# Delta-rule attention and a GELU layer on one core: both tiles turned in one run, the last product in a bank of its own, and VectorE's order laid out anew

## The chip, the core and the metric

The kernel runs on one core of a Trainium2 chip. The core's engines work side by side, each on a queue of its own: TensorE (PE; PEld is its loading of weights) multiplies, VectorE (DVE), ScalarE (ACT) and GpSimd (POOL) work element by element, and SyncE (SP) issues the loads and stores. The metric is the device time of one execution in microseconds (us). Before the change it is 666.46 us, the median of three runs (665.81 to 667.63).

## The reference

`q`, `k`, `v` are (4, 8, 768, 48) and `beta` is (4, 8, 768), all float32. The output of the first part is the input of the second.

```python
k_n = k / (np.linalg.norm(k, axis=-1, keepdims=True) + 1e-06)
for t in range(S):                      # 768 tokens, in order
    y[:, :, t] = einsum('bhd,bhde->bhe', q[:, :, t], state)
    v_old = einsum('bhde,bhd->bhe', state, k_n[:, :, t])
    state = state + beta_t * einsum('bhd,bhe->bhde', k_n[:, :, t], v[:, :, t] - v_old)
x = y.transpose(0, 2, 1, 3).reshape(3072, 384)
h = x @ w_in                            # 384 x 2048
out = (0.5 * h * (1 + erf(h / sqrt(2)))) @ w_out        # 2048 x 384
```

## The kernel before

**Tiling.** The 768 tokens are cut into NC = 12 chunks `c` of 64. A tile, in the code a unit `u` = (c, a) with a = 0 or 1, holds the 64 tokens of a chunk for two of the four batches: 128 partitions. Inside a chunk the recurrence is solved by a triangular inverse, between chunks a state `St` is carried. Two chunks make a group `g`.

**What a chunk needs.** Its keys and queries are transposed (`Kt`, `Qt`: L348/L349 by TensorE and ScalarE, L354/L359 by VectorE). `grams` (psG, L369) multiplies keys with keys, `queries` (L405, P) keys with queries. The norms of the keys: `prep` calls `squares` (ScalarE squares into `ksq`, L277; VectorE adds up into `n`, L280) and takes a root on GpSimd; `finish` calls `factors` (four operations of VectorE, L264 to L268), which make beta over the squared norm, `gm`. `scale_v` (L331, GpSimd) scales v. The inverse of a group is made on VectorE: L437 and L442 lay out the blocks, then 30 pairs of L449 (`tmp`) and L451 (`Nu`) eliminate row by row, L460 (`XM`) and L464 (`Zf`) transpose back. Three "joins" (`join_run`, psJ, L541, with L553 on VectorE and the copies L520 on ScalarE) put the blocks together.

**State steps of a chunk.** `against_state` (psK, L615), `subtract` (L627 on ScalarE, `W` by L628 and L629 on VectorE), `solve` (psU, L645; ScalarE copies `U`), `outputs`: `use` (psY, L664 and L673), `next_state` (St, L678) and `read` (x, L688). Then `turn`, once a tile: TensorE transposes x by three matmuls (psX, L709), ScalarE copies them to `xT` (L710).

**The MLP of a chunk** works on `xT` with 256 tokens. From c = 2 on both layers are cut into blocks and multiplied by a scheme with fewer products, in which VectorE adds and subtracts blocks. First layer: per half b of the columns 11 products of about 0.9 us in the order P1, P5, P6, P2, R22, R11, P7, P3, R12, P4, R21 (L829, in `part_of_layer`). Between them are `mix_x` (L799: TX, needed by P5), the sums L852 and L853 after P6, L861 after P7, L872 after P4, and ScalarE's copies of partial sums into `pu` and its GELUs (L817). Second layer: seven products of 2.6 us in the order 1, 5, 2, 6, 4, 7, 3 (L774, in `two`; 3 is called V here). `mix` prepares operands: n = 1 is L888 (`S`, needed by product 5) and L889, n = 2 is L891, n = 3 is L893. `read2` adds up the results: L922 after 6; L925 (`p`), L926, L927, L931 and ScalarE's L930 after 7; L936 after 3. The weights' sums that this needs are made once, in `sum_of_w_in` (`Sw`), `sums_of_w` (`T`, L757) and `last_sum_of_w` (L761).

**Buffers.** PSUM is handed out by tags. "dn" has two buffers of two banks, used by the state steps, joins and grams; "mlp" has two of one bank, used by X and Y of the products; "sq" and "z" have one bank each after the start, used by V1, Z and the turns. In SBUF the tag "x" (tile x of `read`) has two buffers, "ksq" one.

**Order.** Each step has a due time in units of a stage, written by hand into `plan` by `at(first, last, steps)`, which spreads steps over a stretch in proportion to their weights. `emit` sorts all steps by due time and traces them. In the main part VectorE runs exactly in that order. The order on the other engines is set by a scheduler, except where `together` keeps matmuls in one run, `behind` chains the products of the MLP, and `keep` or `keep_in_program_order` holds instructions of ScalarE in the order they are traced.

**Stages.** Stage w runs the state steps of chunk w beside the MLP of chunk w−1; its start is here the first matmul of P1 of the MLP. Even stages have the three joins of a group and the grams of chunks w+2 and w+3, odd stages the most of an elimination. Chunks 0 to 2 form the start, in which weights are also decoded; after w = 11 only the MLP of c = 11 is left.

Of the kernel before, what the change touches and what calls it, by code (L numbers as in the profile page):

```python
# [16 lines left out]
def kernel(  # L17
# [28 lines left out]
    nc = tc.nc  # L46
# [223 lines left out]
    def squares(u, n, engine=None):  # L270
        kd = u.Kn[:, :, 0:D]
        if engine is nc.gpsimd:
            ksq = su.tile([128, H, D], F32, tag="w_e", name="ksq")
        else:
            ksq = wk.tile([128, H, D], F32, tag="ksq", name="ksq", bufs=1)
        if engine is None:
            nc.scalar.activation(ksq, kd, ACT.Square)  # L277
        else:
            engine.tensor_tensor(ksq, kd, kd, op=ALU.mult)
        nc.vector.tensor_reduce(n, ksq, axis=AX.X, op=ALU.add)  # L280
# [12 lines left out]
    def prep(c):  # L293
# [4 lines left out]
        if c > 3:  # L298
            ns[c] = wk.tile([128, NA, H], F32, tag="n", name="n", bufs=4)
# [10 lines left out]
    def finish(c):  # L310
        t = (c % 2) * NA
        factors(gms[c // 2][:, t:t + NA], beta_m[:, c], ns[c])
# [398 lines left out]

    def state_steps(c, first=(), second=()):
        us = [tiles[c, a] for a in range(NA)]
        steps = [(3.0, together, (against_state, us), *first),
                 (2.0, together, (solve, us), *second), (3.0, outputs, us)]
        return steps + [(0.5, turn, u) for u in us]
# [36 lines left out]
    def sums_of_w():  # L753

        for n, a, b in ((1, B12, B11), (2, B22, 1), (4, B21, 2)):
            T[n] = more[0].tile([128, FH, DH], F32, name=f"T{n}")
# [62 lines left out]
    def part_of_layer(c, b, n):  # L819
# [30 lines left out]
        elif n == "P6":  # L850
            product(fresh("Y1", "mlp", ps), S1[2], L1["T"][2], True)
            nc.vector.tensor_tensor(L1["Y1"], L1["Y1"], L1["pu"][:, 0], op=ALU.add)  # L852
            nc.vector.tensor_tensor(L1["pu"][:, 1], L1["Y1"], L1["pu"][:, 1], op=ALU.add)  # L853
# [19 lines left out]
        else:  # L873
# [3 lines left out]
            if b == NB - 1:  # L877
                keep(nc.scalar.activation, L1["last"], L1["last"], ACT.Gelu)
                for h in range(2):
                    mix(c, 1, h)  # L880

    def mix(c, n, h):
        fs = slice(h * FH // 2, (h + 1) * FH // 2)
        a11, a12, a21, a22 = (A[a][k][:, fs] for a in range(2) for k in range(2))
        if n == 1:
            if h == 0:
                W2["S"] = more[0].tile([128, FH, 128], F32, tag="S1", name="S1")
# [7 lines left out]
    def two(c, n):  # L895
# [9 lines left out]
        elif n == 6:  # L905
            W2["Y"] = ps.tile([128, 2, DH], F32, tag="mlp", name="psY2")
# [7 lines left out]
        else:  # L914
            W2["V"] = W2["Y"][:, 1] if c < NC - 1 else dn("psV2")[:, 0, 0:DH]
# [26 lines left out]
    def second_layer(c, n):  # L942

        two(c, n)
        if n in (1, 2):
            for h in range(2):
                mix(c, n + 1, h)
# [132 lines left out]
    def late():  # L1080
# [3 lines left out]
        for a in range(NA):  # L1084
# [3 lines left out]
            for c in range(5, NC, 2):  # L1088
                tiles[c, a].Kb = Kb

    plan = [at(c + 1 + 0.25 * (c == 1), c + 2 + 0.25 * (c == 0), ffn_steps(c)) for c in range(NC)]
# [6 lines left out]
    plan += [at(1.08, 1.5, sums), at(1.51, 1.511, [(1.0, prep, c) for c in (2, 3)]), at(1.65, 1.655, [(1.0, finish_both)]), at(3.072, 3.073, [(1.0, finish, 4)]), at(2.725, 2.726, [(1.0, queries, third)]),  # L1098
             at(1.12, 1.6, state_steps(1)),
# [9 lines left out]
             at(2.8, 2.985, state_steps(2)[1:]),  # L1109
             at(2.73, 2.731, [(1.0, prep, 4)]), at(2.8, 2.9, [(1.0, grams, [tiles[4, a] for a in range(NA)])])]  # L1110
    plan += [at(0.995, 1.0, [(1.0, load_v, 2)]), at(2.727, 2.728, [(1.0, sums_of_w)]), at(3.2, 3.21, [(1.0, last_sum_of_w)])]
    plan += [at(c + (0.99 if c == 2 else 0.958), c + (0.991 if c == 2 else 0.959), [(1.0, mix_x, c)]) for c in range(2, NC)]
# [4 lines left out]
    for c in range(4, NC):  # L1117
# [10 lines left out]
        t = c - (0.06 if c % 2 == 0 else 0.15)  # L1128
# [83 lines left out]
```

## Time and profile before

| | before |
|---|---|
| median of three runs | 666.46 us |
| the profiled execution | 667.54 us |
| its span | 665.5 us |
| clock granted to TensorE | 0.985 |
| start of P1 in stages 4, 5, 6, 7 | 226.96, 282.68, 328.22, 382.66 us |
| start of P1 in stages 8, 9, 10, 11, and of the last MLP | 428.20, 483.49, 529.02, 579.49, 624.09 us |

The profile is one execution. A group's line gives its line of code, engine, operation, result and operands, count, busy time, mean time of one in ns and how long its engine was idle just before, with what ended that. A line of the timeline gives start, duration, engine, line, operation and count; in brackets the idle time before it and the instruction that ended it. The waits list sums such idle times by the line that waited and the one that released it.

### The profile page before, as it was taken

What the parts mean: (1) busy time and instruction counts of PE and PEld (TensorE: products, weight loads), DVE (VectorE), ACT (ScalarE), POOL (GpSimd) and SP (SyncE); (2) the same over time, 40 slices, a digit from 0 to 9 for tenths busy, and PEclk for the clock granted to TensorE, in tenths of its full rate; (3) what the DMA queues carried; (4) which work ended last, traced back from release to release, by engine and by line L of the source; (5) the groups of instructions that cost most, each with busy time, mean ns of one, the idle gap of its engine ahead of it and who ended that gap; (6) DMA issues with size and microseconds to landing.
All of it is one profiled execution on the core that took longest, in us unless ns stands there. A gap on an engine that the chain in (4) does not pass through costs nothing.

```text
span 665.5 us, 22152 instructions
## 1 busy us (share of the span) xinstructions
PE 628.6 (94%) x9702; PEld 576.0 (87%) x9702; DVE 503.6 (76%) x1040; ACT 254.1 (38%) x587; POOL 72.5 (11%) x62
## 2 busy tenths in 40 slices
PE   6877999999799899999999999999999999999997
PEld 5666877766699899999999999998899999999997
DVE  7999999999599986769886769886778875445242
ACT  3367744623442146232146232145233144132230
POOL 4051400100411012101012101012101000000000
PEclk9977999999899999999999999999999999999999
DMA  8886654302433234421234321221221210100101
GB/s 126 184 253 176 124 168 119 48 1 52 70 54 56 47 42 76 58 40 26 54 46 76 55 40 27 54 33 26 34 41 27 46 29 2 25 3 2 25 1 25
DMA packets 158433, 39.79 MB, mean 60 GB/s; under 512 B 150016, under 2 KB 153216, under 8 KB 158336
## 3 DMA queue, kind: packets, MB, share of 16 engines
q1 hardware_dynamic: 155344, 36.94, 28.5%
q10 hardware_dynamic: 2992, 1.43, 1.0%
q8 instruction: 76, 1.25, 0.8%
q14 instruction: 21, 0.17, 0.1%
HBM read 33.62 MB, written 4.72 MB: 58 GB/s over the span
## 4 chain that ended last, share of the span: by engine, by line
PE 58%; DVE 29%; issue 4%; ACT 4%; DMA 3%; SPq 1%; POOL 0%; DVEq 0%; ACTq 0%; POOLq 0%
PE psX L774 8%; PE psY L774 8%; PE psY L829 8%; PE psX L829 6%; PE psH L732 4%; PE psZ L774 4%; PE psZ L829 4%; PE psV L829 3%; PE psO L746 3%; DVE tmp L449 3%; DVE Nu L451 3%; PE psK L615 3%; DMA Kp<-in_k_dram 2%; PE psG L369 2%; PE psJ L541 2%
## 5 line engine op out<-in xcount | busy, mean ns | idle before, releaser
L829 PE MATMUL psX<-xT,w_in_sb 128*128 128x128 f32 x480 | 65.6, 280 | 0.5 <-ACT pu L817 0.2
L451 DVE TENSOR_TENSOR Nu<-Nu,tmp 128x30 f32<-128x30 f32 (+9 forms) x180 | 59.8, 332 | 6.2
L449 DVE TENSOR_TENSOR tmp<-Nu 128x30 f32<-128x30 f32 (+9 forms) x180 | 60.3, 335 | 4.2
L829 PEld LDWEIGHTS psX<-xT,w_in_sb 128*128 128x128 f32 x480 | 59.5, 193 | 1.9 <-ACT pu L817 1.0
L774 PE MATMUL psY<-w_out_sb,G 128*128 128x192 f32 x304 | 54.1, 329 | 4.4 <-DVE p L925 3.8
L710 ACT COPY xT<-psX 128x384 f32<-128x384 f32 x24 | 11.4, 477 | 118.6 <-PE psX L709 118.5
L774 PE MATMUL psX<-w_out_sb,G 128*128 128x192 f32 x320 | 55.7, 327 | 0.0
L774 PEld LDWEIGHTS psY<-w_out_sb,G 128*128 128x128 f32 x304 | 49.1, 190 | 6.5 <-DVE p L925 6.5
L305 POOL TENSOR_TENSOR n<-n,half 128x16 f32<-128x16 f32 x10 | 30.0, 3001 | 220.7 <-DVE n L280 200.5
L774 PEld LDWEIGHTS psX<-w_out_sb,G 128*128 128x128 f32 x320 | 51.8, 190 | 0.3
L732 PE MATMUL psH<-xT,w_in_sb 128*128 128x256 f32 x192 | 45.1, 388 | 2.0 <-ACT G L734 1.9
L746 PE MATMUL psO<-w_out_sb,G 128*128 128x384 f32 x128 | 44.7, 493 | 0.4 <-DVE w_out_sb L235 0.4
L732 PEld LDWEIGHTS psH<-xT,w_in_sb 128*128 128x128 f32 x192 | 36.0, 192 | 9.1 <-ACT G L734 3.3
L829 PE MATMUL psY<-xT,w_in_sb 128*128 128x128 f32 x320 | 42.4, 275 | 0.0
L817 ACT COPY pu<-psZ 128x512 f32<-128x512 f32 x40 | 23.4, 584 | 41.2 <-PE psZ L829 31.1
L829 PEld LDWEIGHTS psY<-xT,w_in_sb 128*128 128x128 f32 x320 | 38.9, 192 | 0.1
L746 PEld LDWEIGHTS psO<-w_out_sb,G 128*128 128x128 f32 x128 | 23.4, 190 | 14.8 <-DVE w_out_sb L235 1.3
L852 DVE TENSOR_TENSOR psY<-psY,pu 128x512 f32<-128x512 f32 x20 | 14.0, 699 | 28.1 <-PE psY L829 28.1
L817 ACT ACTIVATE G<-G 128x512 f32<-128x512 f32 x40 | 25.2, 629 | 22.0 <-DVE G L861 21.1
L331 POOL TENSOR_TENSOR V<-V,n 128x384 f32<-128x384 f32 x18 | 17.3, 973 | 122.0 <-DMA V<-in_v_dram 98.6
L774 PE MATMUL psZ<-T,S 128*128 128x192 f32 x160 | 28.6, 332 | 1.6 <-DVE S L888 1.6
L893 DVE TENSOR_TENSOR G<-G 128x512 f32<-128x512 f32 x20 | 13.8, 692 | 20.5 <-PE psX L774 20.4
(171 smaller groups left out, 1325.4 us busy)
## 6 DMA issues: line engine op xcount, KB each, us to landing
Kp<-in_k_dram SPq DMA_DIRECT2D x76, 96.0 KB, 3.2
w_out_sb<-in_moe_w_in_dram SPq DMA_DIRECT2D x24, 256.0 KB, 4.5
w_raw<-in_moe_w_out_dram SPq DMA_DIRECT2D x16, 384.0 KB, 4.5
V<-in_v_dram SPq DMA_DIRECT2D x48, 96.0 KB, 3.2
out_dram<-o_sb SPq DMA_DIRECT2D x36, 96.0 KB, 2.2
Qp<-in_q_dram SPq DMA_DIRECT2D x64, 32.0 KB, 2.1
Qp<-in_q_dram SPq DMA_DIRECT2D x16, 96.0 KB, 4.2
Qp<-in_k_dram SPq DMA_DIRECT2D x32, 32.0 KB, 2.4
```

The costliest lines, as they stand in the source:

```text
L305: nc.gpsimd.tensor_tensor(flat, flat, half, op=ALU.pow)
L331: engine.tensor_tensor(u.V, u.V, ns[u.c][:, u.a].unsqueeze(2).to_broadcast([128, H, D]), op=ALU.mult)
L449: nc.vector.tensor_tensor(tmp, nu[:, j + 1:, j:j + 1].to_broadcast([128, n, j]), nu[:, j:j + 1, 0:j].to_broadcast([128, n, j]), op=ALU.mult)
L451: nc.vector.tensor_tensor(nu[:, j + 1:, 0:j], nu[:, j + 1:, 0:j], tmp, op=ALU.add)
L615: nc.tensor.matmul(u.psK[to, x, r, j, :], lhsT=(u.Qt if x else u.Kt)[rows, p, j, :], rhs=St[rows, u.a, p ^ r, j, :], start=True, stop=True)
L732: nc.tensor.matmul(psH, lhsT=w_in_sb[:, f // 2, m, f % 2 * 128:(f % 2 + 1) * 128], rhs=xTs[c][:, m, :], start=(m == 0), stop=(m == NM - 1))
L746: nc.tensor.matmul(u.psO, lhsT=G[:, f, u.a * 128:(u.a + 1) * 128], rhs=w_out_sb[:, f, :], start=(f == 0), stop=(f == NF - 1))
L774: nc.tensor.matmul(ps_, lhsT=lhs[:, f, :], rhs=rhs[:, f, :], start=first and f == 0, stop=f == FH - 1, skip_group_check=not first)
L817: tc.keep_in_program_order(fn(*args))
L829: nc.tensor.matmul(ps_[:, i], lhsT=lhs[:, f // 2, f % 2 * 128:(f % 2 + 1) * 128], rhs=rhs, start=first and i == 0, stop=True, skip_group_c ...
L852: nc.vector.tensor_tensor(L1["Y1"], L1["Y1"], L1["pu"][:, 0], op=ALU.add)
L893: nc.vector.tensor_tensor(a12, a12, a11, op=ALU.subtract)
```

## The change

1. **Norms.** `ksq` takes a buffer of the tag "x" in place of its own, and its ScalarE instruction is held in program order. The sums `n` of two chunks share one tile, and `finish` runs once a group on 128x32 elements, not once a chunk on 128x16.
2. **Turns.** The new `turns` transposes both tiles into one "dn" buffer by six matmuls in one run, followed by one copy of 128x768 on ScalarE, held in order. Chunks 1 and 2 keep a `turn` for each tile. `state_at` gives each state step a due time of its own; weights go.
3. **Sums of the second layer's weights.** `sum_of_w` makes T1 and T2 at 2.727; T4 and the last sum move to 3.595 (from 2.727 and 3.2).
4. **Steps cut out of the MLP.** L853 becomes `add_p5`; `mix(c, 1, 0)` and `mix(c, 3, ·)` get due times of their own. They had followed P6, R21 and product 2.
5. **Buffers.** `S` is written into the tile `pu`, no longer into a tile of its own under the same tag. The result of product 3 is in a "dn" buffer for every chunk, and no longer beside that of product 7.
6. **Due times.** Most steps on VectorE, ScalarE's copies of joins and grams (now in blocks of four or two), some loads and the norms are moved.

The scheduler's order on TensorE changes with it: product 5 of even stages comes after psU, psJ and psG; the six transposes of the turns stand between product 7 and product 3, which isn't interrupted any more; psK of even stages no longer breaks product P4. In the start, `use` of chunk 2 goes ahead of the last matmuls of the MLP of chunk 1 (psO, L746), the transposes L348 of chunk 3 behind P6, and P1 isn't interrupted.

```diff
         else:
-            ksq = wk.tile([128, H, D], F32, tag="ksq", name="ksq", bufs=1)
+            ksq = wk.tile([128, H, D], F32, tag="x", name="ksq")
         if engine is None:
-            nc.scalar.activation(ksq, kd, ACT.Square)
+            keep(nc.scalar.activation, ksq, kd, ACT.Square)
         else:
...
-        if c > 3:
-            ns[c] = wk.tile([128, NA, H], F32, tag="n", name="n", bufs=4)
+        if c > 3 and c % 2 == 0:
+            n = ns["pair"] = wk.tile([128, 2 * NA, H], F32, tag="n", name="n")
+            ns[c], ns[c + 1] = n[:, 0:NA], n[:, NA:]
...
     def finish(c):
-        t = (c % 2) * NA
-        factors(gms[c // 2][:, t:t + NA], beta_m[:, c], ns[c])
+        factors(gms[c // 2], beta_m[:, c:c + 2].rearrange("q c a h -> q (c a) h"), ns["pair"])
...
+    def turns(us):
+        c = us[0].c
+        xT = xTs[c] = wk.tile([128, NM, NA * 128], F32, tag="xT", name="xT")
+        psX = dn("psX")[:, :, 0:DM].rearrange("q a (m n) -> q a m n", n=128)
+        for u in us:
+            for m in range(NM):
+                nc.tensor.transpose(psX[:, u.a, m, :],
+                                    u.x.rearrange("q h d -> q (h d)")[:, m * 128:(m + 1) * 128], ident)
+        keep(nc.scalar.copy, xT.rearrange("q m (a n) -> q a m n", n=128), psX)
+
     def state_steps(c, first=(), second=()):
         us = [tiles[c, a] for a in range(NA)]
-        steps = [(3.0, together, (against_state, us), *first),
-                 (2.0, together, (solve, us), *second), (3.0, outputs, us)]
-        return steps + [(0.5, turn, u) for u in us]
+        return [(together, (against_state, us), *first), (together, (solve, us), *second),
+                (outputs, us), (together, (turns, us))]
...
-    def sums_of_w():
+    def sum_of_w(*which):
 
         for n, a, b in ((1, B12, B11), (2, B22, 1), (4, B21, 2)):
+            if n not in which:
+                continue
...
         elif n == "P6":
             product(fresh("Y1", "mlp", ps), S1[2], L1["T"][2], True)
             nc.vector.tensor_tensor(L1["Y1"], L1["Y1"], L1["pu"][:, 0], op=ALU.add)
-            nc.vector.tensor_tensor(L1["pu"][:, 1], L1["Y1"], L1["pu"][:, 1], op=ALU.add)
...
             if b == NB - 1:
                 keep(nc.scalar.activation, L1["last"], L1["last"], ACT.Gelu)
-                for h in range(2):
-                    mix(c, 1, h)
+                mix(c, 1, 1)
+
+    def add_p5():
+        nc.vector.tensor_tensor(L1["pu"][:, 1], L1["Y1"], L1["pu"][:, 1], op=ALU.add)
...
         if n == 1:
             if h == 0:
-                W2["S"] = more[0].tile([128, FH, 128], F32, tag="S1", name="S1")
+                W2["S"] = L1["pu"].rearrange("q e f n -> q (e f) n")
...
         elif n == 6:
-            W2["Y"] = ps.tile([128, 2, DH], F32, tag="mlp", name="psY2")
+            W2["Y"] = ps.tile([128, 1, DH], F32, tag="mlp", name="psY2")
...
         else:
-            W2["V"] = W2["Y"][:, 1] if c < NC - 1 else dn("psV2")[:, 0, 0:DH]
+            W2["V"] = dn("psV2")[:, 0, 0:DH]
             product(W2["V"], A[0][1], B22, True)
...
-        if n in (1, 2):
+        if n == 1:
             for h in range(2):
-                mix(c, n + 1, h)
+                mix(c, 2, h)
         elif n in (6, 7, 3):
             read2(c, n)
...
+    def state_at(c, *times, first=(), second=()):
+
+        steps = state_steps(c, first, second)
+        if len(times) > len(steps):
+            steps = steps[:-1] + [(turn, tiles[c, a]) for a in range(NA)]
+        return [(t, step) for t, step in zip(times, steps) if t is not None]
...
+    plan += [at(1.08, 1.5, sums), at(1.51, 1.511, [(1.0, prep, c) for c in (2, 3)]), at(1.65, 1.655, [(1.0, finish_both)]), at(2.725, 2.726, [(1.0, queries, third)]),
+             state_at(1, 1.2, 1.333, 1.467, 1.547, 1.573),
...
-             at(2.8, 2.985, state_steps(2)[1:]),
-             at(2.73, 2.731, [(1.0, prep, 4)]), at(2.8, 2.9, [(1.0, grams, [tiles[4, a] for a in range(NA)])])]
-    plan += [at(0.995, 1.0, [(1.0, load_v, 2)]), at(2.727, 2.728, [(1.0, sums_of_w)]), at(3.2, 3.21, [(1.0, last_sum_of_w)])]
-    plan += [at(c + (0.99 if c == 2 else 0.958), c + (0.991 if c == 2 else 0.959), [(1.0, mix_x, c)]) for c in range(2, NC)]
+             state_at(2, None, 2.772, 2.851, 2.906, 2.922),
+             at(2.728, 2.729, [(1.0, prep, 4)]), at(2.8, 2.9, [(1.0, grams, [tiles[4, a] for a in range(NA)])])]
+    plan += [at(0.995, 1.0, [(1.0, load_v, 2)]), at(2.727, 2.728, [(1.0, sum_of_w, 1, 2)]), at(3.595, 3.596, [(1.0, last_sum_of_w), (1.0, sum_of_w, 4)])]
+    plan += [at(c + 0.958, c + 0.959, [(1.0, mix_x, c)]) for c in range(2, NC)]
...
-        t = 3.2 if c == 4 else c - (1.12 if c % 2 == 0 else 0.9)
+        t = 3.2 if c == 4 else c - (0.72 if c % 2 == 0 else 0.9)
         plan += [at(t, t + 0.01, [(1.0, load_blocks, c, "Qb", q)])]
-        t = c - (2.1 if c % 2 == 0 else 2.7) if c > 5 else {4: 2.1, 5: 2.74}[c]
+        t = c - (2.1 if c % 2 == 0 else 2.62) if c > 5 else {4: 2.1, 5: 2.74}[c]
...
-        t = c - (0.06 if c % 2 == 0 else 0.15)
+        t = c + (0.002 if c % 2 == 0 else 0.23)
         plan += [at(t, t + 0.01, [(1.0, turned_q, u) for u in us])]
...
+    for c in range(2, NC):
+        for b in range(NB):
+            t = c + 1 + (0.1 if c % 2 and b == 0 else 0.06 + 0.2576 * b)
+            plan += [at(t, t + 0.001, [(1.0, add_p5)])]
+        plan += [at(c + 1.42, c + 1.421, [(1.0, mix, c, 1, 0)]),
+                 at(c + 1.715, c + 1.716, [(1.0, mix, c, 3, h) for h in range(2)])]
...
-                         at(w - 0.16, w - 0.15, [(1.0, prep, w + 2)]),
-                         at(w + 0.074, w + 0.075, [(1.0, finish, w + 2)])]
-                plan += rows_of(2, w, ((1, 0.08, 0.081), (2, 0.18, 0.2), (6, 0.22, 0.31), (4, 0.385, 0.5),
-                                       (5, 0.5, 0.745), (16, 0.765, 1.02), (1, 1.09, 1.095),
+                         at(w, w + 0.001, [(1.0, prep, 5)]),
+                         at(w + 0.1, w + 0.101, [(1.0, finish, 4)])]
+                plan += rows_of(2, w, ((1, 0.102, 0.103), (2, 0.16, 0.2), (4, 0.224, 0.31),
+                                       (2, 0.325, 0.365), (1, 0.395, 0.4), (2, 0.485, 0.5),
+                                       (2, 0.508, 0.54), (5, 0.6, 0.685), (9, 0.76, 0.94),
...
             elif two_ahead:
-                plan += rows_of(w // 2 + 1, w, ((1, -0.26, -0.25), (1, -0.22, -0.21), (1, -0.2, -0.19),
-                                                (4, -0.15, -0.02), (9, 0.09, 0.31), (3, 0.385, 0.5),
-                                                (4, 0.5, 0.745), (11, 0.765, 1.0), (1, 1.09, 1.095),
+                plan += rows_of(w // 2 + 1, w, ((1, -0.295, -0.294), (1, -0.34, -0.339),
+                                                (1, -0.23, -0.229), (6, -0.22, -0.11),
+                                                (1, -0.07, -0.06), (3, 0.005, 0.05),
+                                                (3, 0.068, 0.148), (2, 0.156, 0.215),
+                                                (2, 0.235, 0.31), (3, 0.325, 0.365),
+                                                (1, 0.398, 0.409), (2, 0.485, 0.5),
+                                                (1, 0.508, 0.54), (5, 0.6, 0.685),
+                                                (2, 0.76, 0.8), (1, 1.0925, 1.093),
                                                 (1, 1.16, 1.161), (1, 1.166, 1.167)))
-            plan += [at(w + 0.25, w + 0.95, state_steps(w, (), query(w)))]
+            plan += [state_at(w, w + 0.367, w + 0.59, w + 0.72, w + 0.93, second=query(w))]
         else:
             j0, j1, j2 = join_steps(w // 2)
             plan += [at(w + 0.165, w + 0.166, [(1.0, together, j0, *query(w))]),
                      at(w + 0.37, w + 0.371, [(1.0, together, j1, *gram(w + 2))]),
-                     at(w + 0.35, w + 0.97, state_steps(w, (), [j2] + gram(w + 3)))]
-            plan += spread("join", 2, w + 0.4, w + 0.425)
-            plan += spread("join", 4, w + 0.66)
+                     state_at(w, w + 0.465, w + 0.58, w + 0.72, w + 0.93, second=[j2] + gram(w + 3))]
+            plan += spread("join", 4, w + 0.373)
+            plan += spread("join", 4, w + 0.64)
             if two_ahead:
-                plan += spread("gram", 1, w + 0.385, w + 0.42, w + 0.54, w + 0.58)
-                plan += spread("gram", 1, w + 0.66, w + 0.661, w + 0.7, w + 0.701)
-                plan += [at(w + 0.25, w + 0.26, [(1.0, prep, w + 2)]),
-                         at(w + 0.5, w + 0.51, [(1.0, finish, w + 2)])]
-            if w + 3 < NC:
-                plan += [at(w + 0.45, w + 0.46, [(1.0, prep, w + 3)]),
-                         at(w + 0.66, w + 0.67, [(1.0, finish, w + 3)])]
+                plan += spread("gram", 2, w + 0.38) + spread("gram", 2, w + 0.42)
+                plan += spread("gram", 4, w + 0.63)
+                plan += [at(w + 0.366, w + 0.367, [(1.0, prep, w + 2)]),
+                         at(w + 0.56, w + 0.561, [(1.0, prep, w + 3)]),
+                         at(w + 0.7, w + 0.701, [(1.0, finish, w + 2)])]
```

More of the change, by code (lines that the diff above doesn't have):

```diff
@@ L1097 @@
     sums = [(1.0, sum_of_squares, tiles[c, a], h) for c in (2, 3) for a in range(NA) for h in range(H)]
-    plan += [at(1.08, 1.5, sums), at(1.51, 1.511, [(1.0, prep, c) for c in (2, 3)]), at(1.65, 1.655, [(1.0, finish_both)]), at(3.072, 3.073, [(1.0, finish, 4)]), at(2.725, 2.726, [(1.0, queries, third)]),
-             at(1.12, 1.6, state_steps(1)),
+    plan += [at(1.08, 1.5, sums), at(1.51, 1.511, [(1.0, prep, c) for c in (2, 3)]), at(1.65, 1.655, [(1.0, finish_both)]), at(2.725, 2.726, [(1.0, queries, third)]),
+             state_at(1, 1.2, 1.333, 1.467, 1.547, 1.573),
              at(1.75, 2.43, rows1[:-1]),
@@ L1153 @@
                             + [(1.0, together, *gram(5))]),
-                         at(w - 0.16, w - 0.15, [(1.0, prep, w + 2)]),
-                         at(w + 0.074, w + 0.075, [(1.0, finish, w + 2)])]
-                plan += rows_of(2, w, ((1, 0.08, 0.081), (2, 0.18, 0.2), (6, 0.22, 0.31), (4, 0.385, 0.5),
-                                       (5, 0.5, 0.745), (16, 0.765, 1.02), (1, 1.09, 1.095),
+                         at(w, w + 0.001, [(1.0, prep, 5)]),
[3 more added lines that the diff above has]
+                                       (2, 0.508, 0.54), (5, 0.6, 0.685), (9, 0.76, 0.94),
+                                       (6, 0.97, 1.058), (1, 1.0925, 1.093),
                                        (1, 1.16, 1.161), (1, 1.166, 1.167)))
             elif two_ahead:
-                plan += rows_of(w // 2 + 1, w, ((1, -0.26, -0.25), (1, -0.22, -0.21), (1, -0.2, -0.19),
-                                                (4, -0.15, -0.02), (9, 0.09, 0.31), (3, 0.385, 0.5),
-                                                (4, 0.5, 0.745), (11, 0.765, 1.0), (1, 1.09, 1.095),
+                plan += rows_of(w // 2 + 1, w, ((1, -0.295, -0.294), (1, -0.34, -0.339),
[6 more added lines that the diff above has]
+                                                (2, 0.76, 0.8), (1, 1.0925, 1.093),
                                                 (1, 1.16, 1.161), (1, 1.166, 1.167)))
-            plan += [at(w + 0.25, w + 0.95, state_steps(w, (), query(w)))]
+            plan += [state_at(w, w + 0.367, w + 0.59, w + 0.72, w + 0.93, second=query(w))]
         else:
```

## The prediction

> **What bounds the kernel now.** I read the page's busy shares first, then its chain, then a table of stages, then the waits of TensorE, then the timeline around each long wait. The first two, from the page:
>
> ```profile
> PE 628.6 (94%) x9702; PEld 576.0 (87%) x9702; DVE 503.6 (76%) x1040; ACT 254.1 (38%) x587; POOL 72.5 (11%) x62
> ...
> PE 58%; DVE 29%; issue 4%; ACT 4%; DMA 3%; SPq 1%; POOL 0%; DVEq 0%; ACTq 0%; POOLq 0%
> ```
>
> TensorE is nearly full, and the chain still runs through VectorE for 29%: products stand behind results of VectorE. Where, shows in the table by stage, whose bounds are the starts of product P1 (window; us, then busy time and instructions of PE, PEld, DVE, ACT, POOL; clock; DMA share; GB/s):
>
> ```profile
> 177.00:227.00 50.00, 47.69 (x741) 46.08 (x740) 44.14 (x102) 15.96 (x33) 5.68 (x5) 0.98 0.31 52
> 226.96:282.68 55.72, 52.86 (x936) 49.99 (x935) 43.56 (x94) 24.09 (x48) 9.33 (x5) 1.00 0.39 59
> 282.68:328.22 45.54, 45.42 (x680) 44.39 (x679) 37.08 (x86) 12.63 (x26) 1.93 (x2) 1.00 0.20 37
> 328.22:382.66 54.44, 52.59 (x936) 49.92 (x935) 41.47 (x88) 24.09 (x48) 9.33 (x5) 1.00 0.39 60
> 428.20:483.49 55.29, 52.92 (x937) 50.10 (x936) 41.48 (x88) 23.57 (x47) 9.33 (x5) 1.00 0.21 35
> ```
>
> The odd stage (w=5) is full: 45.42 of 45.54. The even ones (w=4, 6, 8) carry 1.8 to 2.9 us of idle TensorE and more in switches between product and small matmuls. In w=3 VectorE has 44.14 busy of 50: the one stage that it nearly bounds. TensorE's waits over the whole run (us in total, times, longest):
>
> ```profile
> PE psX L709 <- DVE x L688: 4.0, 1, 4.0
> PE psY L774 <- DVE p L925: 3.8, 4, 1.5
> PE psZ L774 <- DVE S L888: 1.6, 3, 0.5
> ```
>
> The first is in the start (c=2), as VectorE's timeline shows:
>
> ```profile
> 161.77 3.55 DVE L757 TENSOR_TENSOR T<-w_out_sb,T 128x1536 f32<-128x1536 f32 x2
> ...
> 168.30 0.55 DVE L280 TENSOR_REDUCE n<-ksq 128x8 f32<-128x384 f32 x1 [1.37 <-ACT ksq L277]
> 171.56 0.55 DVE L280 TENSOR_REDUCE n<-ksq 128x8 f32<-128x384 f32 x1 [2.71 <-ACT ksq L277]
> 172.03 0.55 DVE L678 TENSOR_TENSOR St<-St,psY 128x384 f32<-128x384 f32 x1
> ```
>
> The new state (L678) and x stand behind the sums T and four norms; x is late, and the turn waits 4.0. The second wait is the end of every MLP:
>
> ```profile
> 378.39 0.49 PE L709 MATMUL psX<-ident,x 128*128 128x128 f32 x3
> 379.63 0.92 PE L774 MATMUL psY<-w_out_sb,G 128*128 128x192 f32 x4 [0.75 <-DVE p L925]
> ```
>
> The last product (V) waits for p, though p reads product 7 and V writes other columns.
>
> [...] psY holds V beside Y, and the V product waits for the read of Y (0.75; 1.54 in w=3). [...] L678 at 172.03 follows a norm that it doesn't need. [...]
>
> ```profile
> 182.17 0.67 DVE L267 TENSOR_TENSOR gm<-beta_m,r 128x16 f32<-128x16 f32 x1
> 182.88 0.75 DVE L268 TENSOR_TENSOR gm<-gm,r 128x16 f32<-128x16 f32 x1
> ...
> 181.99 1.61 POOL L331 TENSOR_TENSOR V<-V,n 128x384 f32<-128x384 f32 x2 [6.89 <-DVE n L264]
> ```
>
> These take 0.17 and 0.18 at 184.04, with POOL idle.
>
> **Part by part, against the profiled run (667.54 us, span 665.5).**
>
> *Start.* One T of 1.76 and two of the four norms (with their idle 1.37 and 2.71) leave the place ahead of L678; psO work of 2.8 moves from before `use` to after it, so `use` starts at 162.1, not 164.87. I place L678 at 164.5 (was 172.03), both x done by 167.8, the turns under the psO matmuls: the 4.0 wait is gone. P1 isn't split by psX and psT any more: its halves take .77+.86 against .89 whole, and the second psX .64 against .33, P5 1.18 against .89 — 1.3 together. Gain 5.3. What is late next is P5, on mix_x (four at .29); the psO cover it.
>
> *Stage w=3.* The moved work lands here: T 1.76 and L761 1.67 at 3.595, the norm of 5, and VectorE was at 44.14. Old waits go (P7b on L861 .77, V on p 1.54, P5 on TX .78, P6 on o_sb .33: 3.4). Walking VectorE's new order with the old durations, p ends at 220.4, some 5 after its product: ScalarE's copy of o_sb waits for it, and xT's copy stands behind. So P1 comes only near 222.2 and P5 at 223.3, against 228.80: lead 5.5, that is 0.2 more. Nearly all 3.4 given back.
>
> *Stage w=4.* Its beginning inherits a late VectorE: I find P7 waiting 0.8 for L852 and the join 1.1 for XM (L460), lead 4.6. The rest removes 2.5 (as below). Lead 7.1 at w=5.
>
> *Even stages w=6, 8, 10.* The reads of before, added from the timeline: Z on S .55 to .62, psJ on XM .26, P2 and R22 on ScalarE's pu .6, P6 on o_sb .38, psK breaking P4 .2, p .75 and switches .2; in w=8 psG on Kt .84. The change puts product 5 (Z) behind psU, psJ and psG, 3 us of cover for S (L888, now half of it at +0.42 of the stage); takes the interruption of the V product out; and brings ScalarE's copies in blocks. I find no new wait in the walk: 3.0, 3.9 and 1.4 (w=10 has no grams).
>
> *Odd stages.* p's wait (.29) goes: product 3 has its own bank. VectorE reaches L861 of the second half at 20.19 after P1, and P4 is due at 20.07: new wait about .2. Net +.1 a stage, 0.4. Below nothing is excluded to within .65, if row pairs take .87 as the slowest did, not .75.
>
> *Turn.* Two copies of 128x384 (.477 each) become one of 128x768. No row of that shape; by 128x384 (.477) and 128x512 (.584) the slope is .107 per 128, so .80 (estimate). [...] I take .80; it lies under V (2.6), at both ends. If V's cover went, P1 would wait .8.
>
> *Norms.* Factors on 128x32 once a pair: 4 operations (about .9) fewer in each of three even stages, on VectorE, which isn't the bound there: nothing. ksq now takes a buffer of x, so a norm waits for the turn of the tile before, and x for the norm. ksq is done at 18 and 28 us of a stage and the turn at 50: hidden. L893 (mix 3) is moved off the place where it idled 20.5 us in all:
>
> ```profile
> L893 DVE TENSOR_TENSOR G<-G 128x512 f32<-128x512 f32 x20 | 13.8, 692 | 20.5 <-PE psX L774 20.4
> ```
>
> That idle time is VectorE's, worth nothing alone; it makes room for rows.
>
> *Banks.* V in a "dn" buffer in all stages: two such buffers, the other holds the turn, whose copy ends during V. Nothing; at worst .8. S in pu's place: pu is dead by then; nothing.
>
> *Sum.* 5.3+.2−.9+2.5+3.0+3.9+1.4+.4=15.8. A walk misses waits that only the chip shows: every stage of before has one or two of .2 to .6. I take .4 in each of ten stages, −4, with 0 and −8 as ends. 667.54−11.8=655.7; the median was 1.1 below the profiled run: 654.7, say 655.
>
> **The rivals.**
>
> *R1, the forecast:* 655.
>
> *R2, VectorE's new order binds.* For it: in odd stages L861 has .1 of slack, XM in even stages .6; order is by hand, so one late step delays all behind it. Against: VectorE idles 8 us a stage. P4 late .65 in five odd stages (3.3), XM 1.1 in three even ones (3.3): 15.8−4−6.6=5.2, so 661.
>
> *R3, the walk is right to the end:* 667.54−15.8−1.1=650.6. Against: the stages of before all have small waits that no sum of durations gives.
>
> *R4, slower: ScalarE stands at a norm.* ksq is now kept in program order ahead of p and U in ScalarE's FIFO. It needs the tokens' k, whose load stands on SP's queue behind earlier loads that wait themselves:
>
> ```profile
> SPq L96 <- PE psY L673: 62.0, 10, 15.4
> ```
>
> The load for w+3 can go after the norm of w+2 (18.4 us into the stage), lands at 23.5 by my count of issues, and is needed at 28: 4.5 of slack, and 5 more until `use` is late. Up to 9.5 us late costs nothing; a wait as long as SP's longest (15.4) would cost 5.9 in w=4, 6 and 8, so 655+17.7=672.7. It decides from 14 us late on. Against: SP's long waits are for buffers that the loads in question don't use.
>
> *R5: no net change,* gains of the start lost in w=3 and w=4: 665 to 668.
>
> **How the numbers follow.** R1 .52, R2 .25, R3 .11, R4 .07, R5 .05. The likeliest is 655. The range takes R3 in at the bottom (649.5) and R2 with another 3 of unlisted waits at the top (664); outside are R4, R5 and tails, 2 in 10. A change under 0.3% (2.0 us) can't be told from none. Faster (under 664.5): R1, R3 and most of R2, .84; same .08: R5 and the rest of R2; slower .08: R4.
>
> **What would show it.** The start right: L678 near 164.5, no wait of psX for x. V right: no wait of L774 for p outside w=3. w=3 right: p some 5 us after product 7, P1 near 222. Even stages: 51.4 between P1 starts instead of 54.4 to 55.3; odd 45.4. R2 shows as psY L829 <- G L861 and psJ <- XM, R4 as ScalarE idle on the k load ahead of ksq. I am wrong if VectorE's idle time shrinks while TensorE's waits don't.

## The result, and the profile after

| | before | after |
|---|---|---|
| median, 20 runs each | 667.41 us | 665.04 us |
| ratio, 95% interval | | 0.9968 (0.9959 to 0.9978) |
| profiled execution, its span | 667.54, 665.5 us | 665.89, 664.1 us |

The change gains 2.4 us. Forecast were 655 us, with a range from 649.5 to 664: the direction was right, the size was five times too large.

The table of stages, again from P1 to P1, now of the changed kernel for w=4, 5, 6 (us; busy time and instructions of PE, PEld, DVE, ACT, POOL; clock; DMA share; GB/s):

```profile
224.02:285.01 60.99, 56.63 (x934) 54.20 (x935) 45.55 (x94) 23.27 (x47) 9.61 (x5) 0.92 0.35 54
285.01:330.59 45.58, 45.53 (x678) 44.57 (x679) 37.77 (x92) 12.42 (x25) 1.90 (x2) 1.00 0.23 40
330.59:383.96 53.37, 51.91 (x936) 49.69 (x934) 41.98 (x77) 23.36 (x47) 9.61 (x5) 1.00 0.38 59
```

w=4 has grown from 55.72 to 60.99 us, with the same matmuls and a clock of 0.92: this one stage takes back twice what the whole change gains. w=6 has shrunk from 54.44 to 53.37 only, w=5 not at all (45.54 to 45.58). TensorE's waits of the changed kernel (us in total, times, longest; lines of code count from the new file, so L840 is the old L829 and L785 the old L774):

```profile
PE psY L840 <- DVE pu L892: 5.9, 4, 3.6
...
PE psY L785 <- DVE o_sb L934: 2.0, 1, 2.0
...
PE psX L840 <- DVE Nu L451: 1.4, 1, 1.4
...
PE psG L369 <- DVE Kt L354: 1.0, 3, 0.3
...
PE psX L840 <- ACT xT L828: 0.9, 3, 0.3
```

None of the three waits that the forecast quoted is left. (The profile puts P1's 1.4 in w=4 down to a row pair, L451. P1 reads xT, whose copy ends at 223.96, 0.04 before that row pair, and P1 begins at 224.02.) The first of the new ones was not in the forecast: product P7 waits for `add_p5` (L892), the step that the change cut out. It stands like this on VectorE in w=6:

```profile
333.54 0.70 DVE L863 TENSOR_TENSOR psY<-psY,pu 128x512 f32<-128x512 f32 x1 [1.07 <-PE psY L840]
334.15 2.11 DVE L460 STREAM_TRANSPOSE XM<-Nu 128x1024 f32<-128x1024 f32 x1
336.15 0.67 DVE L892 TENSOR_TENSOR pu<-psY,pu 128x512 f32<-128x512 f32 x1
```

and on TensorE:

```profile
336.87 1.16 PE L840 MATMUL psY<-xT,w_in_sb 128*128 128x128 f32 x8 [0.75 <-DVE pu L892]
```

P7 adds on to psY. L892 reads psY, so P7 may not begin before L892 is done (L892 ends at 336.82, P7 begins at 336.87). The due time of L892 (0.1 of the stage, with b = 0 in even stages) is behind that of XM (0.0925), which takes 2.1 us. Before, L853 came directly behind L852. In w=4 the same wait is 3.64 us, and something comes on top (changed kernel, timeline and then windows of 2 us with TensorE's clock as the third figure from the end):

```profile
233.33 2.07 PE L840 MATMUL psY<-xT,w_in_sb 128*128 128x128 f32 x8 [3.64 <-DVE pu L892]
235.33 1.97 PE L541 MATMUL psJ<-XM,G 32*64 32x64 f32 x32
237.24 1.99 PE L369 MATMUL psG<-Qt,Kt 48*64 48x64 f32 x64
```

```profile
230.00:232.00 2.00, 0.00 (x0) 0.00 (x0) 2.00 (x4) 1.09 (x2) 0.00 (x0) 1.00 0.44 51
...
234.00:236.00 2.00, 2.00 (x19) 1.77 (x20) 0.49 (x1) 0.00 (x0) 0.00 (x0) 0.50 0.42 51
...
240.00:242.00 2.00, 2.00 (x11) 2.00 (x11) 1.05 (x1) 0.17 (x1) 0.00 (x0) 0.50 0.00 0
...
244.00:246.00 2.00, 2.00 (x20) 2.00 (x20) 0.87 (x2) 0.61 (x2) 0.00 (x0) 1.00 0.15 20
```

The product that takes 1.16 us in w=6 takes 2.07 here, and a join that takes 1.15 (experiment 1) takes 1.97: after the wait TensorE runs at half its clock for 10.2 us, from 233.16 to 243.40.

### The profile page after: what moved, and what is told of

Same layout as the page of the kernel before. It is cut to its first block, busy times and chain, and to the rows that moved or that the text cites. A ratio compares the mean times of both kernels' runs of the same rounds, so it can differ in the third digit from the quotient of the medians.

```text
span 664.1 us, 22173 instructions
## 1 busy us (share of the span) xinstructions
PE 627.8 (95%) x9702; PEld 578.2 (87%) x9702; DVE 506.1 (76%) x1024; ACT 250.8 (38%) x578; POOL 72.3 (11%) x62
## 4 chain that ended last, share of the span: by engine, by line
PE 53%; DVE 34%; ACT 5%; issue 5%; DMA 2%; SPq 0%; ACTq 0%; DVEq 0%
PE psX L785 7%; PE psY L840 7%; DVE tmp L449 6%; DVE Nu L451 5%; PE psY L785 5%; PE psO L755 5%; PE psH L741 4%; PE psX L840 4%; PE psV L840 3%; PE psZ L840 3%; PE psZ L785 2%; PE psG L369 2%; PE psV L785 2%; PE psJ L541 2%; ACT diag L520 2%
## 5 line engine op out<-in xcount | busy, mean ns | idle before, releaser
L840 PE MATMUL psX<-xT,w_in_sb 128*128 128x128 f32 x480 | 64.8, 278 | 2.4 <-DVE Nu L451 1.4
L451 DVE TENSOR_TENSOR Nu<-Nu,tmp 128x30 f32<-128x30 f32 (+9 forms) x180 | 60.3, 335 | 6.2
L840 PEld LDWEIGHTS psX<-xT,w_in_sb 128*128 128x128 f32 x480 | 58.7, 192 | 4.6 <-ACT xT L828 3.4
L942 ACT COPY o_sb<-psX 128x192 f32<-128x192 f32 x10 | 3.2, 319 | 150.3 <-PE psX L718 73.6
L306 POOL TENSOR_TENSOR n<-n,half 128x16 f32<-128x16 f32 x10 | 30.0, 3000 | 242.4 <-DVE n L280 222.2
L785 PE MATMUL psX<-w_out_sb,G 128*128 128x192 f32 x320 | 55.3, 326 | 0.0
L785 PEld LDWEIGHTS psX<-w_out_sb,G 128*128 128x128 f32 x320 | 52.1, 190 | 0.0
L840 PE MATMUL psY<-xT,w_in_sb 128*128 128x128 f32 x320 | 43.6, 280 | 5.9 <-DVE pu L892 5.9
L840 PEld LDWEIGHTS psY<-xT,w_in_sb 128*128 128x128 f32 x320 | 39.7, 195 | 6.7 <-DVE pu L892 6.7
L863 DVE TENSOR_TENSOR psY<-psY,pu 128x512 f32<-128x512 f32 x20 | 13.9, 696 | 22.2 <-PE psY L840 22.2
L785 PE MATMUL psY<-w_out_sb,G 128*128 128x192 f32 x160 | 28.1, 329 | 2.3 <-DVE o_sb L934 2.0
L785 PEld LDWEIGHTS psY<-w_out_sb,G 128*128 128x128 f32 x160 | 26.1, 190 | 3.5 <-DVE o_sb L934 3.5
L785 PE MATMUL psY<-T,G 128*128 128x192 f32 x160 | 28.6, 332 | 0.0
L785 PE MATMUL psZ<-T,pu 128*128 128x192 f32 x160 | 28.6, 332 | 0.0
```

The source lines that it names most:

```text
L306: nc.gpsimd.tensor_tensor(flat, flat, half, op=ALU.pow)
L451: nc.vector.tensor_tensor(nu[:, j + 1:, 0:j], nu[:, j + 1:, 0:j], tmp, op=ALU.add)
L785: nc.tensor.matmul(ps_, lhsT=lhs[:, f, :], rhs=rhs[:, f, :], start=first and f == 0, stop=f == FH - 1, skip_group_check=not first)
L840: nc.tensor.matmul(ps_[:, i], lhsT=lhs[:, f // 2, f % 2 * 128:(f % 2 + 1) * 128], rhs=rhs, start=first and i == 0, stop=True, skip_group_c ...
```

## The experiments

Each was timed beside the kernel before on the same chip (its medians there: 667.05 to 667.56 us). The changed kernel takes 665.0 us. Kernel 1 is that of experiment 1.

**1. add_p5 ahead of XM.** One due time of the changed kernel:

```diff
-            t = c + 1 + (0.1 if c % 2 and b == 0 else 0.06 + 0.2576 * b)
+            t = c + 1 + 0.06 + 0.2576 * b
```

> The changed kernel with one due time altered: add_p5 of even stages stands ahead of XM (L460) again, directly behind L863, as in the kernel before. Changed kernel: 665.0 us. Theory A (P7 writes the psY that add_p5 reads, so it waits for add_p5, and add_p5 stands behind the 2.0 us of XM; and the long wait in w=4 lowers TensorE's clock afterwards): P7's wait of 0.75 goes in w=6, 8, 10, the join psJ waits up to 0.4 for XM instead; in w=4 the wait falls from 3.64 to about 1.8 and the matmuls behind it take their usual time again (psJ 1.1 instead of 1.97). About 658 us. Rival B (the slow matmuls of w=4 don't come from the wait): 662 us, psJ in w=4 still near 2 us. Rival C (XM's lateness costs what P7 gains): 664 to 665 us.

Measured: 657.7 us, ratio 0.9871 (0.9851 to 0.9891). Theory A holds. TensorE at the same place of w=4:

```profile
230.83 1.16 PE L840 MATMUL psY<-xT,w_in_sb 128*128 128x128 f32 x8 [1.97 <-DVE pu L892]
231.82 0.61 PE L840 MATMUL psV<-xT,Sw 128*128 128x128 f32 x4
232.94 1.15 PE L541 MATMUL psJ<-XM,G 32*64 32x64 f32 x32 [0.50 <-DVE XM L460]
```

The wait is 1.97, the join takes its 1.15, and w=4 is 55.16 us long. Of the 5.8 us gained there, 1.2 are waits (3.64 less 1.97 less 0.50); the other 4.6 are TensorE's busy time (56.63 us at a mean clock of 0.92 in the changed kernel, 51.98 at 1.00 here). w=6, 8 and 10 lose their 0.75, get 0.2 of psJ's wait for XM and are 0.74 to 0.77 shorter. So one due time costs three times what the whole change gains.

**2. The moved sums.** T4 and the last sum of the weights back where they were, and, in a second kernel, in gaps of VectorE in the start (the edit of the second):

```diff
-    at(3.595, 3.596, [(1.0, last_sum_of_w), (1.0, sum_of_w, 4)])
+    at(2.956, 2.957, [(1.0, sum_of_w, 4)]), at(2.99, 2.991, [(1.0, last_sum_of_w)])
```

> The changed kernel with the sums T4 and L772 at the places that they had before the change (2.727 and 3.2). Theory A (VectorE is full from the middle of w=3 to the beginning of w=4, and the 3.5 us of the two sums moved there make it late for product 7, P1 and P7): the waits 2.03, 1.36 and most of 3.64 go, and with the last the slow matmuls; the start has slack for T4. About 655 us. Rival B (the sums only move the lateness: the start loses 1.8 and W or P4 in w=3 about 1): 658 us. Rival C (VectorE is late for another reason): 664 to 666 us.

> The changed kernel with T4 at 2.956 and L772 at 2.99, in the two gaps of 1.8 and 2.7 us that VectorE has between the state step of chunk 2 and the norm of chunk 5. Theory A (w=3 is bound by VectorE's sum of work): Y's wait of 2.03, P1's of 1.36 and most of P7's 3.64 in w=4 go, and with the last the slow matmuls behind it: 655 us. Rival B (these waits come from the order of the row pairs, not from the amount of work): 662 to 665 us. If the slow matmuls have another cause than the wait: 659 us.

Measured: 662.5 us (0.9927, 0.9915 to 0.994) and 661.1 us (0.9917, 0.9902 to 0.9932). Product 7 of w=3 no longer waits, and P1 waits 0.31 and 0.42 instead of 1.36. But P7 of w=4 waits 3.61 and 3.65 as before, and takes 2.08 behind it in both, the join 1.97; in the second kernel the clock is at 0.50 there (230 to 238 us). Theory A was right on w=3 and wrong on w=4: there the order at the head of the stage (two row pairs, Qt, three row pairs, L863, XM, then L892) makes P7 late, however early VectorE arrives: from P1 to L863 it takes 6.1 us in the changed kernel and in the second one alike.

**3. Both at once.**

> Both edits of the runs before at once: add_p5 ahead of XM (657.7 us alone) and the two sums in VectorE's gaps of the start (661.1 alone, 3.9 less than the changed kernel). Theory A (two separate losses: a wait of P7 and a full VectorE in w=3): they add up, 653.8 us, with no wait of product 7 in w=3 and no half clock anywhere after the start. Rival B (one and the same lateness of VectorE): about 657 us.

Measured: 656.7 us, 0.985 (0.9834 to 0.9867), its runs from 654.6 to 659.2. By the median that is rival B's number. The profiled run, the fastest, shows what becomes of the gain: w=3 is 3.4 us shorter than in kernel 1 (51.67 to 48.23), but P7 still waits 1.98 in w=4 and the clock halves for 3.4 us behind it (P7 takes 1.65, the join 1.80), which it doesn't in the profile of kernel 1 (1.16 and 1.15); w=4 is 1.2 longer. So theory A was right on two separate losses and wrong on "no half clock anywhere after the start".

**4. The bank alone,** on the kernel before: `psY2` with one part, `W2["V"] = dn("psV2")[:, 0, 0:DH]` for every chunk.

> The kernel before (667.4 us) with one part of the change alone: the result of product 3 always in a dn buffer, Y in a tile of its own. Theory A: the waits of V for p go (0.75 in w=4, 6, 8; 1.54 in w=3; 0.29 in odd stages), nothing takes their place: 662 us. Rival B (xT's copy or VectorE's TX is late instead, since V is earlier by as much): 664 to 667 us. Rival C: no gain, 667.4, if the dn buffer has to be waited for.

Measured: 663.5 us, 0.9942 (0.9929 to 0.9954): more than the whole change gains. Its windows for w=5 and w=6:

```profile
282.62:327.77 45.15, 45.15 (x680) 44.36 (x679) 37.24 (x89) 12.64 (x26) 1.85 (x2) 1.00 0.20 36
327.77:381.22 53.45, 52.46 (x936) 49.83 (x935) 40.99 (x85) 24.03 (x48) 9.33 (x5) 1.00 0.40 62
```

An odd stage is 0.39 shorter than before, an even one 1.0. Only w=4 is longer (57.65): P5 waits 2.57 for TX there, and the clock falls to 0.50 behind it (230 to 232 us; P5 takes 1.69, the next product 1.92). In the changed kernel odd stages have lost this gain again. Set beside this kernel from P1 on, its w=5 is 0.11 late from P5 on, where P1 had waited for xT, and another 0.32 late once the second half's P4 has begun at 20.40 and not at 20.07, when L871 had ended (20.34).

**5. The norms undone,** on kernel 1: `ksq` in a buffer of its own and not held in order, one sum a chunk, factors twice. Then only its buffer, then only the factors:

```diff
-            ksq = wk.tile([128, H, D], F32, tag="x", name="ksq")
+            ksq = wk.tile([128, H, D], F32, tag="ksq", name="ksq", bufs=1)
```

> As add_p5 ahead of XM (657.7 us), with the norms undone: ksq in a buffer of its own and not held in order, one sum for each chunk, the four operations of factors twice for a pair. Theory A (the forecast's: VectorE isn't the bound there, so the shorter factors bring nothing): 657.7 us within 0.7. Rival B (they stand on VectorE between the grams and the new state of even stages, where product 7 already waits .15 for the sum behind that state): .9 in each of w=4, 6, 8, so 660.4 us.

> As add_p5 ahead of XM (657.7 us), with one part of the norms undone: ksq in a single buffer of its own instead of the two of the tokens' tiles; order held, one sum for the pair, factors once. Theory A (with one buffer the second square waits for VectorE's sum of the first, and in ScalarE's queue U, the grams and the joins stand behind it; this is what made the kernel with all of the norms undone slow, 672.3): at least half of those 14.6 us, 665 us or more. Rival B (the doubled factors on VectorE made it slow): 658 us.

> As add_p5 ahead of XM (657.7 us), with the factors of a pair made in two sets of four operations on 128x16 again instead of one on 128x32; ksq, order and sums as changed. Theory A (ksq's buffer is what counts): the second set of about .8 stands on VectorE ahead of the new state in w=4, 6, 8 and delays product 7 by .8 there: 660 us. Rival B (VectorE isn't the bound there): 657.7 within .7. Rival C (it makes the 14.6 us): 668 us or more.

Measured: 672.3 (1.0072, 1.006 to 1.0085), 672.5 (1.0081, 1.0067 to 1.0095) and 660.4 us (0.9899, 0.9882 to 0.9915). The single buffer alone costs as much as all of it, 14.8 us. How, shows in w=6 of that second kernel, on ScalarE and VectorE:

```profile
369.57 0.52 ACT L828 ACTIVATE ksq<-Kp 128x384 f32<-128x384 f32 x1 [2.07 <-DVE n L280]
370.11 0.31 ACT L652 COPY U<-psU 64x192 f32<-64x192 f32 x1
370.45 0.59 ACT L520 COPY G<-psG 128x512 f32<-128x512 f32 x1
```

```profile
372.83 1.98 DVE L437 STREAM_TRANSPOSE Nu<-diag 128x1024 f32<-128x1024 f32 x1 [2.15 <-ACT diag L520]
```

The second square waits 2.07 for VectorE to sum up the first; the last copy of U and the grams stand behind it in ScalarE's queue; VectorE waits for diag, and product 7 1.8 us for what follows. w=6 and w=8 are 2.35 us longer than in kernel 1. More is lost elsewhere: 5.2 in the start, where the second square waits 4.55 for a sum that stands behind T on VectorE, with the copies of G and diag behind it, and TensorE's `use` waits for diag:

```profile
167.06 1.10 PE L664 MATMUL psY<-U,P 64*64 64x48 f32 x32 [4.17 <-ACT diag L380]
```

The clock is at 0.50 from 165.89 to 172.72 there: this product takes 1.10 and the other half of `use` 1.07 (0.68 and 0.65 in experiment 4), the eight psO matmuls behind them 4.70 (2.85 in kernel 1). Another 5.1 is lost in w=4, where product 7 waits 1.8 too and the clock halves for 6.8 us behind P7's wait of 1.99 (psG takes 1.99), which it doesn't behind the 1.97 of kernel 1 (psG 1.16). The two spells of 6.8 us at half the clock hold back 6.8 us of work at most (an estimate), so up to half of the 14.8 is clock. The factors made twice cost 2.6 us in all: product 7 waits 0.80 for L934 in the same three stages, as theory A of the third kernel said. With all of the norms undone they don't come on top.

**6. The norms alone,** on the kernel before.

> The kernel before (667.4 us) with the norms' part of the change alone: ksq in the tokens' buffers and held in order, one sum for a pair, factors once. Theory A (in the order of before, where U, grams and joins have slack on ScalarE, it is worth little but in the start, whose norms no longer wait for each other): start earlier by 1 to 3, the rest as before, 665 us. Rival B (the second buffer is worth as much as it is in the new order): 655 us or less. Rival C (holding ksq in order costs): over 668 us.

Measured: 659.7 us, 0.9886 (0.9871 to 0.99). All three theories missed: the norms' part is worth 7.8 us even in the old order. VectorE in w=6 of the kernel before, and of this one:

```profile
356.48 0.54 DVE L280 TENSOR_REDUCE n<-ksq 128x8 f32<-128x384 f32 x1
357.67 0.56 DVE L280 TENSOR_REDUCE n<-ksq 128x8 f32<-128x384 f32 x1 [0.64 <-ACT ksq L277]
```

```profile
350.52 1.01 DVE L280 TENSOR_REDUCE n<-ksq 128x8 f32<-128x384 f32 x2
```

With one buffer VectorE stood still between the two sums, ahead of L872 and S. With two it doesn't, and the wait of product 5 for S (0.54 in w=6) is gone with no change of TensorE's order. Stages w=4, 6 and 8 are 1.4 to 1.7 us shorter (w=6: 53.04), w=3 is 1.0 shorter, and the start gains 2.8. That the second buffer does this, and not the shorter factors, is read from the trace; in this order the buffer was not tried alone.

**7. Norms and bank together,** on the kernel before.

> The kernel before with two parts of the change, norms (659.7 us alone) and the bank of its own for product 3 (663.5 alone), and nothing else. Theory A (the two act at different places, U and grams in the middle of even stages and p at the end of all): the gains of 7.8 and 3.9 add up, 655.9 us, and all other parts of the change together cost 9. Rival B (with the norms' gain, VectorE's TX is late at w=4 as it was with the bank alone, and the clock falls after it): 657.5 to 659 us.

Measured: 657.2 us, 0.9851 (0.9835 to 0.9867). The gains add up but for 1.5 us: in w=4 P5 waits 2.49 for TX, as rival B said. The rest of the change, put on top of these two parts, makes the kernel 8 us slower.

**8. The turns undone,** on kernel 1: three transposes and one copy for each tile.

> As add_p5 ahead of XM (657.7 us), with the turns of the two tiles undone: three transposes and a copy of 128x384 for each, as before the change, one of them inside product 3. Theory A (the merged turn saves two switches of TensorE of about .1 each in every stage and nothing else): 659.5 us. Rival B (its one copy of .8 makes P1 wait .29 in even stages, which goes with two copies): 657 us or less.

Measured: 659.1 us, 0.9887 (0.9866 to 0.9908), its runs from 658.2 to 663.5; kernel 1 has 657.7, from 657.1 to 660.4. By the medians the merged turn is worth 1.4 us, theory A's size, but the two intervals overlap. The profiled run is the slowest, 663.5 us, and loses 3.0 in the start and 3.9 in w=4 (P5 waits 1.27 for TX, and the clock halves for 6.8 us behind P7's wait of 1.99, the join taking 1.97 and psG 1.99), so only its later stages are set beside kernel 1: w=5, 7 and 9 are 0.36 longer (45.94), w=6 and 8 0.34 and 0.31 shorter (52.29 in w=6), since P1 doesn't wait for xT. Both theories are at work. Why the merged turn brings no more shows on ScalarE at the end of w=6 of the changed kernel:

```profile
382.89 0.32 ACT L942 COPY o_sb<-psX 128x192 f32<-128x192 f32 x1 [14.31 <-issue]
383.11 0.81 ACT L828 COPY xT<-psX 128x768 f32<-128x768 f32 x1
```

The transposes were done at 381.1. The copy of xT starts at 383.1, behind that of o_sb, which stands behind L937 and L938 and these behind six row pairs.

**9. Every wait that is left.** The edits of experiments 1 and 2 together (sums in the gaps), and: Kt (2.49 to 2.515 stages ahead), one row pair of odd stages behind L871, XM ahead of L863 in w=6, 8, 10, in w=3 three row pairs and for even chunks Qt behind `add_p5`, the copy of o_sb behind that of xT.

> Those two edits and small ones of due time or order against each wait that the changed kernel still shows: XM before L863 at the head of w=6, 8, 10; three row pairs of w=3 and Qt of even chunks behind add_p5; Kt (L354) ahead of L900; one row pair of odd stages behind L871; ScalarE's copy of o_sb behind that of xT. Theory A (what is left of TensorE's waits is VectorE's and ScalarE's order, and each goes when its producer is moved): waits of psJ .2, psG .32, P1 .29 and P4 .23 go, even stages 52.0 and odd ones 45.2 us: 648 us. Rival B (they reappear at the next consumer): 652 to 654 us.

> The sum of the edits again (add_p5 ahead of XM; T4 and L772 in VectorE's gaps of the start; XM, Kt, row pairs and ScalarE's copy of o_sb moved), with Qt of even chunks at 0.095 of the stage, before the next chunk's queries are loaded into the same buffer, and two row pairs of odd stages behind the first L871. The earlier version took 650.9 us. Theory A (each wait goes with its producer): odd stages 45.3 instead of 45.63, even ones 51.4: 650 us. Rival B (waits come back elsewhere): 652 us or more.

> The sum of the edits once more, without the last one (two row pairs of odd stages behind the first L871), which gave P4 a wait of .42. Theory A (odd stages go back to 45.63, three of them .32 shorter): 651 us, the fastest so far. Rival B (the 650.9 of the first version came from Qt being read at another time): 652.5 us.

Measured: 650.9 us (0.9756, 0.9743 to 0.9768), 652.3 (0.9774, 0.976 to 0.9788) and 649.9 (0.9743, 0.9726 to 0.9761). In the first, Qt of even chunks comes after the load of the next chunk's queries into its buffer, so part of its output belongs to other tokens; the work is the same. The second has two row pairs too many behind the first L871 and a new wait of 0.42 in odd stages. The third is the fastest, 17 us below the kernel before. Its stages w=5 and w=6:

```profile
272.87:318.50 45.63, 45.52 (x679) 44.52 (x679) 38.05 (x94) 12.41 (x25) 1.78 (x2) 1.00 0.23 40
318.50:369.92 51.42, 51.38 (x936) 49.68 (x935) 41.47 (x75) 23.47 (x47) 9.62 (x5) 1.00 0.39 61
```

TensorE is busy for 51.38 of 51.42 us: no wait is left there. Odd stages still have 0.5 that the bank alone doesn't have: 0.11 from P7 on, and 0.37 at the first half's P4, which begins 8.42 us after P1 and not 8.04, when L871 has ended (8.36).

## Why the prediction was wrong

**The step that failed is "Stage w=4. Its beginning inherits a late VectorE: I find P7 waiting 0.8 for L852 and the join 1.1 for XM (L460), lead 4.6."** P7 waits for L892, the last reader of the psY on to which it adds, and not for L852; L892 is one XM of 2 us further back in VectorE's order. The wait that the walk did see was too small as well: with L892 directly behind L863 it is still 1.97 in w=4. Forecast for w=4 was a gain of 1.6 us (lead 5.5 to 7.1), measured is a loss of 5.3 (55.72 to 60.99). The same omission made "I find no new wait in the walk" wrong for w=6, 8 and 10. Experiment 1 moves this one step: 657.7 us, 2.7 from the forecast. Product 7's wait of 2.03 in w=3 is of the same kind: it adds on to the psY that L934 reads.

**A wait was priced at its length.** The clock behind it was left out. Behind P7's 3.64 us of waiting in the changed kernel it stood at 0.50 for 10.2 us, in which TensorE was busy for 10.07, and waits of 2.57 and 1.99 us had half the clock behind them too (last section).

**Start.** L678 was forecast at 164.5 and came at 164.61, and the 4.0 wait went. The lead is 3.6 at psG (180.99 to 177.43), not 5.3. TensorE stood 1.64 inside `use` with no releaser in the profile, and in other kernels of the series 0.5 to 1.6 or not at all; its cause is open. The 1.3 that I charged to P1's split halves belongs to the clock, which was 0.50 at 176 to 178 us in the kernel before, behind its 4.0 wait. They came all the same, since the changed kernel's clock is at 1.00 there (from 60 to 233 us): the size was right by luck.

**Stage w=3** was right in its size and in its chain (p late, then o_sb, then xT): a lead 0.2 larger was forecast, and it goes from 3.6 to 3.8 at P5 (228.80 to 225.01). P1 came at 224.02, forecast "near 222.2", and the 1.8 are nearly what the start lacked (1.7). Product 7's 2.03 was not in the walk. That the sums belong elsewhere (experiment 2, 3.9 us) could have been read off the same walk.

**Even stages.** Forecast 3.0, 3.9 and 1.4, measured 1.07, 1.93 and 0.52. Each lost P7's 0.75, and w=6 and w=8 also psG's 0.32 for Kt and P1's 0.29 for xT. The 0.84 that w=8 had over w=6 before went, as forecast: both are 53.37 now. 51.4 was the forecast length of an even stage; 51.42 is measured where these waits are gone (experiment 9).

**Odd stages.** The new wait of P4 for L871 (the old L861), forecast at about 0.2, is 0.22. The 0.11 behind P1's wait for xT was not in the walk: w=5, 7 and 9 are 0.04 longer and not 0.1 shorter; w=11 is 0.39 shorter.

**Norms:** "on VectorE, which isn't the bound there: nothing" was wrong. I counted the four operations saved (experiment 5: 0.8 in three stages) and not the second buffer. The whole part is worth 7.8 us alone. The wait of Z for S that I meant to hide by TensorE's order goes with this part, without that order (experiment 6).

**Turn:** the copy takes 0.81, as estimated from the two shapes measured (0.80). "it lies under V" holds in odd stages; in even ones it starts too late.

**Banks:** the wait for p goes everywhere, as forecast, worth 3.9 alone.

**Rivals.** What came is R5's number, gains of the start lost in w=3 and w=4, at .05. Its place was half right (w=4, not w=3), and its cause was not named: R2 had the mechanism (VectorE's order, by hand) but looked at P4 and XM.

## What to carry to other kernels

Before a step that reads an accumulator is moved in an order by hand, list every reader that the next product into that accumulator must wait for, not only its operands; what stands ahead of the reader delays the product as soon as it exceeds the slack (the 2.1 us of XM cost P7 0.75 in w=6 and 1.67 in w=4). Time the parts of a large change alone: here the norms with their second buffer and the bank of product 3 bring 10 us, and the rest costs 8, of which two due times give back nearly all (656.7 us in experiment 3). Count a buffer by the queues that stand behind the one who waits for it, and not by the operations that it saves.

## What the runs showed of the hardware

Some waits of TensorE cost more than themselves here: the clock fell to 0.50 behind waits of 4.00 (before, start), 3.64 (changed kernel), 3.65 (experiment 2, second kernel) and 2.57 us (experiment 4), and stayed there for 3.4 us (4.00 and 2.57) or 10.2 us (3.64 and 3.65). Behind the 3.61 of experiment 2's first kernel the matmuls show the same: P7 2.08, the join 1.97, psG 1.99. The length of the wait alone doesn't tell it: in kernel 1 the clock was 0.51 from 216 to 218 us, behind a wait of 1.99 in w=3, and 1.00 from 228 to 236, around one of 1.97 in w=4. In the changed kernel a wait of 2.03 at the same product as the former left the clock at 1.00.

The low clock behind a wait lasts 3.41 us in the traces, 6.83 (experiment 5) or 10.24. Here are stretches of 3.41 us in kernel 1: one ahead of its fall, the next, and one with most of the wait of 1.97 (TensorE's busy time is the first figure behind the comma, the clock the third from the end):

```profile
212.65:216.06 3.41, 1.42 (x9) 1.12 (x8) 3.28 (x11) 0.00 (x0) 0.00 (x0) 1.00 0.00 0
216.06:219.47 3.41, 3.41 (x13) 3.41 (x12) 3.13 (x9) 0.00 (x0) 0.00 (x0) 0.50 0.02 5
229.71:233.12 3.41, 1.79 (x18) 1.63 (x20) 3.31 (x4) 1.09 (x2) 0.00 (x0) 1.00 0.41 49
```

Behind the stretch with 1.42 us of work the clock halves, behind the one with 1.79 it doesn't; 3.41 us of the changed kernel that hold most of the wait of 2.03 (212.68 to 216.09) have 1.82, and it doesn't there. But in the first kernel of experiment 9 a stretch with 1.79 was followed by half the clock (at 229.95; psG, begun at 229.46, took 1.62, not 1.16). What decides whether the clock falls, and whether it is back after 3.4 or 10.2 us, was not shown: no run tried it by itself.
